# Attention, Fourier mixing and an MLP on one core: q, k and v cast in their transfer by GpSimd's queue, and the second MLP product of all chunks from seven block products

## The chip, the core and the metric

The kernel runs on one core of a Trainium2 chip. The time is the device time of one execution in microseconds (us). A run of the kernel is compared with runs of the kernel before on the same chip.

## The reference, cut to what matters

For 4 batches of 768 positions and 8 heads of 64, a causal attention with a window of 96 and 8 global keys makes x. The real part of a two-dimensional Fourier transform of x is added to it, the rows are normalised, and an MLP of width 2048 is added:

```python
scores = q @ k.T / 8 - slopes[:, None, None] * dist      # dist: |i - j|, 96 for a global key out of the window
a = softmax(where(is_global | is_local, scores, -1e9))
x = (a @ v).transpose(0, 2, 1, 3).reshape(4, 768, 512)
u = x + real(fft(fft(x, axis=1), axis=2))
un = (u - mean(u)) / sqrt(var(u) + 1e-6)
out = u + relu(un @ w_ch1) @ w_ch2                       # w_ch1 [512, 2048], w_ch2 [2048, 512]
```

q, k, v and the two weights are given in fp32; all products are made in fp16 with fp32 sums.

## The kernel before

The order of all work is made at build time by a list scheduler, `Plan` (L23). Work of PE stands in four streams: MIX (the Fourier part), ATT (attention), PH (first MLP product) and PG (second one, taken strictly in order). Work of the other engines and of the DMA queues is handed to `later` with the engines that may do it and an assumed cost for each. `run` (L153) walks through both and always takes what can start first by its own clock, corrected by hand-set offsets (`BIAS`), and by assumed landing times (`LAND`). What comes out is one fixed instruction list for each engine, executed in order, with semaphore waits between engines. DMAs rotate over eight semaphores, so that an issue waits for the eighth one before it.

**Loads.** A head pair's q, k or v is 384 KB in fp32. All 68 such DMAs are issued by the sync engine (SP), in `load` (L362) and `run_dma` (L407). They land as fp32 in buffers that are free for now: those of hT (the hidden activations), u, qs, and for batch 1 those of the weights w1 and w2. An engine then casts each to fp16: q and k in `cast_qk` and `cast_direct` (ACT L411, DVE L413, POOL L415), v of batches 0 and 1 in `cast_v0` (POOL L456), v of batches 2 and 3 in `cast_v` (POOL L501). The weights are loaded by POOL's queue as eight DMAs of 512 KB that cast in the transfer (`wload` L1467, issues L1472 and L1477). A small DMA, `hold` (L1484), stands in SP's queue until the last piece of w2 has landed; the loads of batches 2 and 3 stand behind it.

**Attention.** Keys are kept in an order in which the even positions of a block of 128 come ahead of the odd ones. For batches 0 and 1, `v_place` (L460) brings v into that order by 12 matmuls of 64x128 per head pair (L472), through PSUM, with a copy on DVE (L490) and one on ACT (L491). With two of the units stand 24 matmuls on zeros (L465). q and k are transposed by PE in `trans` (48 transposes of 64x64 per pair, L583; copies DVE L594 or ACT L598) for batches 0 and 1, and by DMA in `trans_dma` (L550; one full and two half transposes per pair, SP) for batches 2 and 3. Scores (`score` L605) of batches 0 and 1 get their distance bias by a matmul (L629) and go through exp (ACT L665). Those of batches 2 and 3 go through exp (L662) and are multiplied by exp of the bias, `mk`, on DVE (L677). `mk` is made by eight exps of a table `dist_k`, which POOL copies (L1431). Products with the global keys (`glob` L711, from `kG`, POOL copies L544) and with v (`av` L750, L765 and L776) follow.

**Fourier part and MLP.** x goes out to DRAM and comes back in another row order (`bounce` L805). The transform is folded and multiplied (`fold_s`, `fold_d`, `y_unit` L987), mirrored by POOL copies (`mirror` L1022 to L1035) and multiplied again (`u_unit` L1067); u is added up by DVE (L1086, L1095), un made by ACT (L1117), 1/std by POOL (L1133, L1134). Per batch there are three chunks of 256 rows, twelve in all. A chunk's first product is `ph_unit` (L1188, 64 matmuls of 256 columns, relu on ACT L1194 or DVE L1195). Its second product is, for the first eight chunks, `pg_unit` (L1212, 32 matmuls of 512 columns; the result is added to u by DVE, L1221). For the last four (`CS = 8`) it is made from seven products of 2x2 blocks instead of eight (`pg_units`, 56 matmuls of 256 columns, L1293; adds L1311). This takes sums of blocks of w2, made once (`w2_sums` L1239), and of hT for each chunk (`s_sums` L1253), all by DVE. The sums stand in space of `mk` and of the exp buffers that batch 3's attention no longer needs.

Of the kernel before, what the change touches and what calls it, by code (L numbers as in the profile page):

```python
# [14 lines left out]
P = 128  # L15
# [7 lines left out]
class Plan:  # L23
# [8 lines left out]
    LAND = {("xw", 0, 0): 34.0, ("xw", 0, 1): 36.0, ("xr", 0): 41.0, ("ld", 4, 2): 47.7, ("ld", 5, 2): 53.4, ("ld", 6, 2): 58.9, ("ld", 7, 2): 64.7, ("w1", 0): 44.6, ("w1", 1): 48.2, ("w1", 2): 52.2, ("w1", 3): 55.8, ("w2", 0): 59.5, ("w2", 1): 63.6, ("w2", 2): 66.6, ("w2", 3): 69.1}  # L32
    LAT = {"ACT": 0.14, "DVE": 0.12, "POOL": 0.08}

    def __init__(self):
        self.t = {"PE": 0.0, "ACT": 0.0, "DVE": 0.0, "POOL": 0.0, "SP": 0.7, "DMA": 1.9, "DMA2": 0.0}
        self.tok = {}
        self.ready = []
        self.pending = []
        self.rings = {}  # L40
        self.left = {}
        self.n = 0
        self.lanes = [0.0] * 8

# [23 lines left out]
    def later(self, ways, needs=(), after=0.0, outs=(), uses=(), ring=None, lat=0.0, dma=0.0, then=None, rank=1, nd=None):  # L68

        self.n += 1  # L70
        if nd is None:
            nd = int(dma > 0 and ways[0][0] in ("SP", "ACT"))
        self.pending.append((self.n, ways, list(needs), after, outs, uses, ring, lat, dma, then, rank, nd))
        self.promote()
# [11 lines left out]
    def first(self):  # L86

        best = None
        for i, (ready, p) in enumerate(self.ready):
            if p[11]:  # L90
                ready = [max(r, self.lanes[p[11] - 1]) for r in ready]
            c = (min(max(self.t[w[0]], r) for w, r in zip(p[1], ready)) - self.AHEAD * (p[10] < 0) + self.BIAS.get(p[4][0] if p[4] else None, 0.0),
# [4 lines left out]

    def emit(self, place):
        ready, (_, ways, needs, after, outs, uses, ring, lat, dma, then, _, nd) = self.ready.pop(place)
        if nd:  # L100
            ready = [max(r, self.lanes[nd - 1]) for r in ready]
# [14 lines left out]
        for _ in range(nd):  # L116
            self.lanes.append(max(end + lat, self.t[eng] + 2.2, *[self.LAND.get(o, 0.0) for o in outs]))
            self.lanes.pop(0)
# [4 lines left out]
        self.promote()  # L123

# [9 lines left out]
    def slot(self, tag):  # L134
# [7 lines left out]
    BIAS = {(1, 5): -0.7, ('ss', 1, 1): -3, (2, 27): -0.7, ('ex', 1, 3, 2): -3, (1, 46): -0.7, ('qk', 10, 1): -1.5, ('c', 't1'): 1.5, ('w1', 2): 3,  # L142
            ('er', 4): -0.7, ('ss', 2, 0): 0.7, ('h', 6, 6): 3, ('qk', 5, 0): 3, ('qkT', 6): -0.7, ('c', 't2'): 0.3, ('ex', 1, 2, 0): -0.7,
            ('xb', 11, 2): -1.5, ('h', 6, 5): 3, ('ss', 2, 1): 0.7, ('qkT', 10): -0.7, ('ex', 0, 2, 1): -1.5, (3, 13): 0.7, (1, 42): 0.7,
            ('un', 7, 0): -0.7, ('s', 11, 3): 0.7, ('x', 0, 3, 2): -1.5, ('qk', 9, 0): 1.5, ('qk', 7, 1): -0.7, ('qk', 0, 0): 1.5,
            ('ld', 15, 1): 1.5, ('h', 5, 1): 0.3, ('h', 5, 4): 0.3, ('qk', 11, 1): 0.7, (3, 73): -1.5, ('un', 0, 1): -1.5, ('y', 1, 2, 0): 3,
            ('er', 2): 0.3, ('qkT', 8): 0.7, ('h', 8, 4): -1.5, ('w1', 0): 3, ('vc', 2): 0.7, (1, 36): 0.3, (3, 47): 0.3, ('ld', 8, 1): -1.5,
            ('ob', 11, 1): -3, ('qkT', 14): 0.7, ('er', 19): -0.3, ('h', 8, 0): -1.5, (1, 92): -0.7, ('kG', 14, 0): 0.3, ('u', 5, 0): 0.3,
            ('w2t', 0): 0.3, ('z', 3, 0): 3, (1, 64): -1.5, ('v', 0, 2, 0): -0.3, ('ss', 6, 1): 3, (2, 21): -1.5, (2, 19): 0.3, ('rd', 10, 0): -0.7,
            ('sid', 2): -0.3, (3, 51): -3, (2, 5): -3}  # L150
    AHEAD = 0.0

    def run(self, streams):  # L153

        left = [[(*u, (i, k)) for k, u in enumerate(s)] for i, (s, _) in enumerate(streams)]
        while True:
            best = None
            for i, s in enumerate(left):
                for k, (needs, ring, _, name) in enumerate(s[:self.LOOK if streams[i][1] else 1]):
# [13 lines left out]
                    c = (max(r, self.t["PE"]) + self.BIAS.get(name, 0.0), i, k, g or "", max(r, self.t["PE"]))  # L173
# [37 lines left out]
def kernel(  # L211
# [63 lines left out]
    sel = np.zeros((P, 128))  # L275
    gpos = np.flatnonzero(tau < NG)
    for h in range(4):
        for g in range(NG):
            sel[gpos[g], h * 32 + h * NG + g] = 1.0
# [37 lines left out]
    NBUF = {"hT": 3, "qk": 2, "qs": 3, "qkT": 4, "er": 2, "v0": 2, "eg": 1, "x": 1, "xr": 1, "zy": 1, "eA": 1,  # L317
# [10 lines left out]
    ident = kon.tile([P, 256], FP16, tag="ident", name="ident")  # L328
    sel_sb = ident[:, 128:256]
    idn = ident[:, 0:128]  # L330
    dist_sb = kon.tile([P, 2, NM], FP16, tag="dist", name="dist")
    dist_k = kon.tile([P, NM], FP16, tag="distk", name="distk")
    sid = kon.tile([P, H, P], FP16, tag="sid", name="sid")
# [3 lines left out]
    mk = kon.tile([P, H, NM], FP16, tag="mk", name="mk")  # L337
    W1 = {}
# [4 lines left out]
    v16 = [kon.tile([P, NS, H, 66], FP16, tag=f"v16{i}", name=f"v16{i}") for i in range(2)]  # L343
# [14 lines left out]
    def vat(n):  # L358

        return ("u", min(n, HP)) if n < HP or n == 2 * HP - 1 else ("qs", 2 + n - HP)  # L360

    def load(b, hp, which):  # L362
        n = HP * b + hp
        h0 = 2 * hp
        gate = [("gate",)] if n == FB * HP else []
        if b >= FB:
            srcs = [(0, q), (1, k)] if which == "qk" else [(2, v)]
            for w, src in srcs:
                i = 1 + HP + 3 * (n - FB * HP) + w

                def run(src=src, i=i, w=w):
                    t = stage[("t", n, w)] = buf("qs", i, [P, 2 * NS, Dh], FP32, 1)
                    if w < 2:
                        run_dma(t.rearrange("p (m t) d -> p m (t d)", t=2), src, b, h0)
                        return
                    x = src[b, h0:h0 + 2].rearrange("h s d -> (h s) d").rearrange("(n m t) d -> t m n d", m=64, t=2)
                    for t2 in range(2):
                        nc.sync.dma_start(t[64 * t2:64 * t2 + 64], x[t2])
                pl.later([("SP", 0.55 if w < 2 else 1.1, run)], free("qs", i) + gate, 0.0, [("ld", n, w)], lat=1.7, dma=1.5 if w < 2 else 2.5, nd=1 + (w > 1))
                if w < 2:  # L380
                    cast_direct(b, hp, w, i)
        elif which == "v":
            def run():
                t = stage[("t", n, 2)] = buf(*vat(n), [P, NS, 2 * Dh], FP32, 1)
                run_dma(t, v, b, h0)
            pl.later([("SP", 0.55, run)], free(*vat(n)) + [("xi",)] * (n >= HP), 0.0, [("ld", n, 2)], lat=1.7, dma=1.45)
        else:
            tag, ti, users, slot = (("hT", hp, 2, 0) if hp < 3 else ("qs", 0, 1, None)) if b == 0 else \
                (("w1", "w2")[hp // 2], 0, 4, 2 * (hp % 2))
            for w, src in enumerate((q, k)):  # L390
                at = (tag, ti) if slot is not None else (tag, w)

                def run(w=w, src=src, at=at):
                    if slot is None:
                        t = buf(at[0], at[1], [P, NS, 2 * Dh], FP32, 1)
                    else:
                        if at not in stage:
                            stage[at] = buf(at[0], at[1], [P, users, NS, 2 * Dh], FP32, users)
                        t = stage[at][:, slot + w]
                    stage[("t", n, w)] = t  # L400
                    run_dma(t, src, b, h0)
                pl.later([("SP", 0.55, run)], free(*at), 0.0, [("ld", n, w)], lat=1.7, dma=1.45)
                cast_qk(b, hp, w, at)

    def run_dma(t, src, b, h0):

        nc.sync.dma_start(t, src[b, h0:h0 + 2].rearrange("h s d -> (h s) d").rearrange("(m p t) d -> p m (t d)", p=P, t=2))  # L407

    def copy_on(on, d, s):
        if on == "ACT":  # L410
            A(d, s, AF.Copy)  # L411
        elif on == "DVE":
            V.tensor_copy(d, s)  # L413
        else:
            nc.gpsimd.tensor_copy(d, s)  # L415

    def cast_qk(b, hp, w, at):
        n = HP * b + hp

        def cast(on):  # L420
            if n not in qk16:
                qk16[n] = buf("qk", n, [P, 2, NP, 2, 2, Dh], FP16, 1)
            d = qk16[n][:, w].rearrange("p n t h d -> p (n t) h d")
            s = stage[("t", n, w)].rearrange("p (h n) (t d) -> p h (n t) d", h=2, t=2).rearrange("p h j d -> p j h d")
            copy_on(on, d, s)
        ways = [("ACT", act(768), lambda: cast("ACT"))]
        if b == 0 and not (w and hp):
            ways.append(("DVE", dve2(768), lambda: cast("DVE")))
        elif b == 0:
            ways = [("POOL", 0.87, lambda: cast("POOL"))]  # L430
        else:
            ways.append(("POOL", 0.87, lambda: cast("POOL")))
        pl.later(ways, [("ld", n, w)] + free("qk", n), 0.0, [("qk", n, w)], [("free",) + at], rank=b)

# [25 lines left out]
    def v_place(b, hp):  # L460
        n = HP * b + hp

        def run(start, ring):
            pv = bank(ring, f"pvp_{n}")
            idle = lambda k: [nc.tensor.matmul(pv[:, 1, 3 * P:4 * P], EG[:, 0:P], EG[:, 0:P], start=True, stop=True) for _ in range(k)]  # L465
            if n == 1:
                idle(10)
# [1134 lines left out]
```

The softmax here doesn't subtract the row's maximum and nothing guards it: scores larger than these inputs give would overflow.

## Time and profile before

| what | value |
|---|---|
| median of 3 runs | 263.72 us (263.44 to 265.83) |
| span of the profiled execution | 263.7 us |
| PE busy | 246.5 us, 93% |
| DVE, ACT, POOL busy | 173.3, 151.4, 67.2 us |
| first MLP product begins (L1188) | 53.1 us |
| last matmul ends | 259.7 us |
| DMA queues of SP and ACT | 57.3% and 6.8% of 16 engines' time |
| DMA queue of POOL (w1, w2) | 9.8% |

A row of a group of instructions reads: line, engine, operation, result<-operands, shape and type, count | busy us, mean ns of one | idle us of the engine just before them, and what ended most of it. PE is the matmul side of TensorE, PEld its weight load, which overlaps. The chain of waits is the work that ended last, followed back from the end; printed in order of time, each piece has its start, its length, its engine and line. A mean of matmuls is longer than their pace, as they overlap; the pace is read from the chain.

### The profile page before, as it was taken

The page shows a single profiled execution, that of the slowest core. Times are in us where ns is not written, and L with a number is a line of the kernel's source. Part 1 is how long each engine was busy: PE and PEld are TensorE (multiplying, and loading weights), DVE is VectorE, ACT ScalarE, POOL GpSimd, SP SyncE. Part 2 cuts the span into 40 slices and gives each one's busy share as a digit, 9 for nine tenths or more (in the row PEclk, how much of TensorE's full clock was granted, in tenths as well). Part 3 has the DMA queues.
Part 4 walks back from the last instruction along what each step waited for, and adds up shares of the span by engine and source line. Part 5 has one row for each costly group of instructions (what it writes and reads, how often), then busy time and mean ns, then how long its engine had stood idle before and what let it go on. Part 6 is the DMA issues. An engine that isn't in the chain of part 4 may idle for free.

```text
span 263.7 us, 7306 instructions
## 1 busy us (share of the span) xinstructions
PE 246.5 (93%) x3080; PEld 180.6 (68%) x3080; DVE 173.3 (66%) x355; ACT 151.4 (57%) x257; POOL 67.2 (25%) x130
## 2 busy tenths in 40 slices
PE   8678778799999999999999999999999999999993
PEld 2556555578765785776685465677678778888883
DVE  3348999853399536782578958578995935644373
ACT  3276999756647655795682364993544265433300
POOL 1334335980041063514101623011221311000000
PEclk9799999979999999999999999999999999999998
DMA  7999959999699998999999897303641440310222
GB/s 211 296 293 272 309 142 289 225 196 201 125 223 172 283 267 106 183 212 157 218 160 207 205 281 116 90 2 82 145 137 40 23 114 25 83 40 2 80 80 82
DMA packets 76386, 42.02 MB, mean 159 GB/s; under 512 B 33474, under 2 KB 72514, under 8 KB 76354
## 3 DMA queue, kind: packets, MB, share of 16 engines
q1 hardware_dynamic: 69298, 32.65, 57.3%
q0 software_dynamic: 4224, 4.19, 9.8%
q10 hardware_dynamic: 2832, 4.72, 6.8%
q8 instruction: 24, 0.39, 0.6%
q14 instruction: 8, 0.07, 0.1%
HBM read 31.59 MB, written 9.44 MB: 156 GB/s over the span
## 4 chain that ended last, share of the span: by engine, by line
PE 77%; ACT 10%; DVE 5%; DMA 2%; issue 1%; POOL 1%; SPq 1%; DVEq 0%
PE ph L1188 30%; PE pg L1212 21%; PE pgD L1293 5%; ACT ex L665 4%; PE pgA L1293 4%; PE pav L776 4%; PE pu L1067 3%; PE py L987 3%; DMA u<-in_v_dram 2%; PE sc L638 2%; DVE qkT L594 2%; ACT er L662 2%; PE pav L765 1%; ACT un L1117 1%; POOL ww L1035 1%
## 5 line engine op out<-in xcount | busy, mean ns | idle before, releaser
L1188 PE MATMUL ph<-unT,w 128*128 128x256 f16 x768 | 94.7, 276 | 0.0
L1188 PEld LDWEIGHTS <-w 128*128 128x128 f16 x768 | 73.9, 99 | 13.9 <-issue 2.2
L1194 ACT ACTIVATE hT<-ph 128x512 f16<-128x512 f32 x81 | 48.1, 599 | 48.4 <-PE ph L1188 48.3
L1212 PE MATMUL pg<-w,hT 128*128 128x512 f16 x256 | 59.9, 379 | 0.0
L1212 PEld LDWEIGHTS <-hT 128*128 128x128 f16 x256 | 24.3, 98 | 24.7 <-issue 0.6
L662 ACT ACTIVATE er<-sc 128x768 f16<-128x768 f32 (+2 forms) x24 | 21.4, 929 | 6.0 <-PE sc L638 5.9
L665 ACT ACTIVATE ex<-sc 128x992 f16<-128x992 f32 (+2 forms) x24 | 20.6, 937 | 2.1 <-PE sc L641 2.1
L677 DVE TENSOR_TENSOR ex<-er,mk 128x768 f16<-128x768 f16 (+2 forms) x24 | 15.6, 661 | 8.1 <-ACT er L662 7.9
L1133 POOL TENSOR_SCALAR sm<-sm 128x2 f32<-128x2 f32 x12 | 4.4, 368 | 62.8 <-ACT un L1126 62.6
L1221 DVE SCALAR_TENSOR_TENSOR u<-pg,sm,u 128x512 f32<-128x512 f32 x16 | 12.0, 748 | 11.8 <-PE pg L1212 11.8
L1086 DVE SCALAR_TENSOR_TENSOR u<-pu,xr 128x512 f32<-128x512 f32 x18 | 11.7, 688 | 9.0 <-PE pu L1067 9.0
L501 POOL CAST v<-qs 128x768 f16<-128x768 f32 x8 | 6.8, 844 | 40.1 <-DMA qs<-in_v_dram 40.1
L1126 ACT ACTIVATE un<-un 128x512 f16<-128x512 f16 x24 | 15.0, 626 | 3.2 <-DMA unT<-un 1.8
L776 PE MATMUL pav<-v,ex 128*128 128x65 f16 x352 | 16.5, 193 | 0.4 <-ACT ex L665 0.3
L776 PEld LDWEIGHTS <-ex 128*128 128x128 f16 x352 | 15.1, 97 | 2.4 <-issue 1.3
L411 ACT ACTIVATE qk<-qs 128x768 f16<-128x768 f32 x11 | 9.2, 844 | 9.6 <-DMA out_dram<-u 7.0
L1035 POOL COPY ww<-zy 128x512 f16<-128x512 f16 x16 | 9.2, 609 | 21.1 <-PE py L987 17.7
L1195 DVE TENSOR_SCALAR hT<-ph 128x512 f16<-128x512 f32 x15 | 10.3, 688 | 6.1 <-PE ph L1188 6.0
L1117 ACT ACTIVATE un<-u,sm 128x512 f16<-128x512 f32 x13 | 9.2, 720 | 8.7 <-DVE sm L1090 8.5
L1293 PEld LDWEIGHTS <-hT 128*128 128x128 f16 x128 | 12.5, 98 | 1.6
L796 DVE TENSOR_TENSOR x<-pav,rc 128x512 f16<-128x512 f32 (+1 forms) x21 | 12.9, 615 | 0.7
L544 POOL COPY kG<-qkT 64x8 f16<-64x8 f16 x32 | 8.1, 256 | 18.9 <-DVE qkT L594 15.0
(124 smaller groups left out, 382.1 us busy)
## 6 DMA issues: line engine op xcount, KB each, us to landing
out_dram<-u SPq DMA_DIRECT2D x23, 256.0 KB, 2.3
w<-in_moe_w_ch_dram POOLq DMA_DIRECT2D x8, 512.0 KB, 11.2
qs<-in_q_dram SPq DMA_DIRECT2D x9, 384.0 KB, 5.2
qs<-in_k_dram SPq DMA_DIRECT2D x9, 384.0 KB, 5.0
qs<-in_v_dram SPq DMA_DIRECT2D x16, 192.0 KB, 5.0
xr<-xd ACTq DMA_DIRECT2D x3, 768.0 KB, 5.3
u<-in_v_dram SPq DMA_DIRECT2D x5, 384.0 KB, 7.1
w<-in_q_dram SPq DMA_DIRECT2D x4, 384.0 KB, 6.7
```

The source lines that it names most:

```text
L662: A(mine(), cut(pa), AF.Exp, 0.0, 0.125)
L665: A(cut(expst[hp][:, :, g * 512:g * 512 + (384 if g == 2 else 512)]), cut(pa), AF.Exp, 0.0, 0.125)
L677: VT(o, mine(), m, op=ALU.mult)
L776: nc.tensor.matmul(po[:, jj, hh * 65:(hh + 1) * 65], lhsT, v16[b % 2][:, i, h, 0:65], start=(jp == 0 and a == 0), stop=(a == len(ops) - 1) ...
L796: VT(X[b][:, 2 * jp:2 * jp + 2, first * Dh:(first + nh) * Dh].rearrange("p j (h d) -> p j h d", d=Dh), pv[:, :, :, 0:Dh], rc.to_broadcast( ...
L1035: nc.gpsimd.tensor_copy(rev[:, n], T[("y", b)][:, n, :, :, ::-1])
L1126: A(x, x, AF.Square, accum_out=MV[c][:, a, 2:3])
L1188: nc.tensor.matmul(ph[:, a * CH:(a + 1) * CH].rearrange("p (x m) -> p x m", x=2), W1[0][:, d, jb * P:(jb + 1) * P], UNT[c][:, :, d, :], st ...
L1194: pl.later([("ACT", act(512), lambda: A(dst, ph, AF.Relu)), ("DVE", dve(512), lambda: V.tensor_scalar_max(dst, ph, 0.0))], [], e, [("h", c ...
L1212: nc.tensor.matmul(pg, HT[c][:, jb, t * P:(t + 1) * P], W2[0][:, jb, :], start=(jb == 0), stop=(jb == NJ - 1))
L1221: V.scalar_tensor_tensor(UT[c][:, t, :], pg, MV[c][:, t, 3:4], UT[c][:, t, :], op0=ALU.mult, op1=ALU.add)
L1293: nc.tensor.matmul(o, lhs(j), rhs(j), start=(first and j == 0), stop=(j == NK - 1), skip_group_check=True)
```

## The change

1. All q, k and v are loaded by DMAs on POOL's queue that cast from fp32 to fp16 and write straight to where the data is used. v comes as two DMAs per head pair, each with every second position into 64 partitions (768 runs of 256 B). q and k of batches 0 and 1 come as one DMA each (768 runs of 512 B, 16 DMAs), those of batches 2 and 3 as four each (384 runs of 256 B, 64 DMAs). With this the staging buffers, all casts, `v_place` with its copies, the 68 loads of SP and `hold` are gone; 24 matmuls on zeros stay (`idle`). A POOL copy of one cell of batch 0's re-read x (`wgate`) stands ahead of batch 1's v and of w2; q, k and v of batches 2 and 3 are issued after w2.
2. A PE transpose takes all 128 partitions (24 instead of 48 per pair); DMA transposes are 16 full ones instead of 8 full and 16 half ones; q and k have three buffers (`NBUF`) and those of hT.
3. `CS = 0`: all twelve chunks use the block products. The two products that take plain blocks come first (p2, p1), then p45, p6, p7, p3. The tables of w2 and two sums of a chunk have space of their own (`wt`, `sx2`) or that of the distance tables (`first`), free after the last `mk` exp; table t1 overwrites a block of w2, sums s3 and s4 overwrite blocks of hT. Each sum may be made by DVE or POOL: of 48 sums of hT 30 stand on DVE and 18 on POOL, of 8 of w2 5 and 3.
4. `LAND` is empty, and `BIAS` has other entries, which also name groups.

```diff
     def load(b, hp, which):
...
-                pl.later([("SP", 0.55 if w < 2 else 1.1, run)], free("qs", i) + gate, 0.0, [("ld", n, w)], lat=1.7, dma=1.5 if w < 2 else 2.5, nd=1 + (w > 1))
...
+        if which == "v":
+            for t in range(2):
+                def run(t=t):
+                    nc.gpsimd.dma_start(v16[b % 2][64 * t:64 * t + 64, h0:h0 + 2, :, 0:Dh].rearrange("m h i d -> m (h i) d"),
+                                        v[b, h0:h0 + 2].rearrange("h (i m t) d -> t m (h i) d", m=64, t=2)[t])
+                pl.later([("POOL", 0.84, run)], ([("avdone", b - 2)] if b > 1 else []) + order_needs(b, "v"), 0.0, [("v", b, hp, t)],
+                         lat=2.2, dma=0.63, rank=order_rank(b, hp, "v"))
+            return
+        tag, ti = ("hT", n // 2) if n < 6 else ("qk", n - 6)
+        for w, src in enumerate((q, k)):
+            if b >= FB:
+                for x in range(4):
+                    def run(w=w, src=src, t=x // 2, h=x % 2):
...
+                        nc.gpsimd.dma_start(qk16[n][64 * t:64 * t + 64, w, :, h], src[b, h0 + h].rearrange("(i m t) d -> t m i d", m=64, t=2)[t])
+                    pl.later([("POOL", 0.5, run)], free(tag, ti) + order_needs(b, "qk"), 0.0, [("qk", n, w, x)], lat=2.2, dma=0.32, rank=order_rank(b, hp, "qk"))
+                continue
...
+                nc.gpsimd.dma_start(qk16[n][:, w].rearrange("p h n t d -> p (h n) (t d)"),
+                                    src[b, h0:h0 + 2].rearrange("h s d -> (h s) d").rearrange("(m p t) d -> p m (t d)", p=P, t=2))
...
     def trans(b, hp):
...
-                        for a in range(2):
-                            for h in range(2):
-                                r = slice(64 * a, 64 * a + 64)
-                                nc.tensor.transpose(o[64 * h:64 * h + 64, a, w, x, t], src[r, w, x, t, h], idn[r, r],
-                                                    tile_position=(64 * a, 64 * h))
+                        for h in range(2):
+                            nc.tensor.transpose(o[64 * h:64 * h + 64, w, x, t], src[:, w, h, x, t], idn,
+                                                tile_position=(0, 64 * h))
...
     def w2_sums(i):
...
+        both([("w2", 2 + i), ("w2", i)], "t3", lambda: WT(1)[:, k0], lambda: b(1, 1), lambda: b(0, 1), ALU.subtract)
+        both([("t3", i)], "t2", lambda: WT(2)[:, k0], lambda: WT(1)[:, k0], lambda: b(0, 0), ALU.add)
+        both([("t2", i)] + [("mk", hp) for hp in range(HP)], "t4", lambda: WT(0)[:, k0], lambda: b(1, 0), lambda: WT(2)[:, k0], ALU.subtract)
+        both([("t3", i)] + [("plain",)] * (pl.CS > 0), "t1", lambda: b(0, 1), lambda: b(0, 1), lambda: b(0, 0), ALU.subtract)
...
     def s_sums(c):
...
+        both(hs + sfree(0), ("s", c, 1), lambda: new(0), lambda: block(1, 0), lambda: block(1, 1), ALU.add)
+        both([("s", c, 1)] + sfree(1), ("s", c, 2), lambda: new(1), lambda: SX[c, 0], lambda: block(0, 0), ALU.subtract, [("free", "sx", 0, i0)])
+        both([("s", c, 1), ("p1", c)], ("s", c, 3), lambda: block(1, 0), lambda: block(0, 0), lambda: block(1, 0), ALU.subtract)
+        both([("s", c, 2), ("p2", c)], ("s", c, 4), lambda: block(0, 1), lambda: block(0, 1), lambda: SX[c, 1], ALU.subtract, [("free", "sx", 1, i0)])
...
+        PG.append((h1 + [("w2", 2), ("w2", 3)], ("pg",), p2))
+        PG.append((h0 + [("w2", 0), ("w2", 1)], None, p1))
+        PG.append(([("s", c, 1)] + tws("t4") + tws("t1"), ("pg",), p45))
+        PG.append(([("s", c, 2), ("lo", c)] + tws("t2"), None, p6))
+        PG.append(([("s", c, 3), ("ra", c, 1)] + tws("t3"), None, p7))
+        PG.append(([("s", c, 4), ("rd", c)], None, p3))
...
         for i in range(8):
-            needs = [("qk", 7, 1), ("free", "w1", 0)] if i == 0 else [("wl", 3), ("free", "w2", 0)] if i == 4 else [("wl", i - 1)]
+            needs = ([("qk", 7, 1, "i")] if i == 0 else [("wl", i - 1)]) + [("wgate",)] * (i == 4)
...
+        pl.later([("POOL", 0.2, lambda: nc.gpsimd.tensor_copy(cell, XR[0][0:1, 0, 0:2]))], [("xr", 0), ("wl", 3)], 0.0, [("wgate",)], rank=pl.ORD["gate"])
```

## The prediction

> **What bounds the kernel now.** I read the page's first two parts, then a table of windows, then the chain of waits in order of time, then the groups.
>
> ```profile
> PE 246.5 (93%) x3080; PEld 180.6 (68%) x3080; DVE 173.3 (66%) x355; ACT 151.4 (57%) x257; POOL 67.2 (25%) x130
> PE   8678778799999999999999999999999999999993
> DMA  7999959999699998999999897303641440310222
> ```
> PE is not full in the first eight slices (to 53 us) and is full after. The transfers fill the same start, and stay high to slice 25.
>
> ```profile
> 0.00:20.00 20.00, 14.49 (x302) 8.58 (x302) 7.85 (x30) 9.25 (x12) 6.09 (x18) 0.91 1.05 267
> 20.00:40.00 20.00, 15.70 (x528) 11.53 (x530) 17.91 (x43) 17.38 (x26) 7.75 (x18) 1.00 0.92 244
> 40.00:60.00 20.00, 17.28 (x287) 12.84 (x285) 15.52 (x32) 15.38 (x34) 15.62 (x25) 0.91 1.16 232
> 60.00:80.00 20.00, 20.00 (x244) 14.92 (x242) 11.17 (x21) 11.87 (x24) 3.50 (x5) 1.00 0.94 185
> ```
> (Window, length, busy PE, weight load, DVE, ACT, POOL, clock, DMA share, GB/s.) From 20 to 40 DVE and ACT are the full engines (17.9 and 17.4 of 20); from 60 PE is.
>
> ```profile
> 2.87 5.53 DMA u<-in_v_dram
> 8.45 0.83 POOL v L456
> 9.32 0.53 PE pvp L472 x12
> 9.86 1.62 PE pvp L465 x14
> 11.50 0.57 DVE v L490
> 12.10 0.49 ACT v L491
> 12.59 1.76 ACT ex L665 x2
> ...
> 52.16 0.62 ACT un L1117
> 53.14 5.26 PE ph L1188 x32
> ...
> 258.81 0.89 PE pgD L1293 x8
> 259.73 0.48 DVE u L1311
> ```
> The start hangs on v's cast and placing, in front of the first exp (12.59); from the first MLP product (53.14) to the last matmul (259.73) the chain is PE almost without a break. So the time is a start S = 53.1, a PE run of 206.6 and a tail of 263.7 − 259.7 = 4.0. The execution's 263.7 is the median's 263.72, so the sum needs no offset.
>
> **What the Trainium skill says.** "DMA: Bandwidth & Descriptors", section "SWDGE vs HWDGE vs iDMA": a cast in the transfer can only be issued by GpSimd, whose cores write every descriptor. The trace agrees that this takes POOL's time: L1472/L1477 issue w in 0.74 to 0.86 us each, for 512 runs.
> "SBUF — State Buffer", "SBUF: two separate sides": while VectorE runs in a two-port mode, GpSimd can't write descriptors, so that such a DMA starves. The trace doesn't show it: four w issues took 2.98 us at 51.6 while DVE had work for 15.5 of 20 us. But those are eight issues; the change has 120.
> "DMA: Bandwidth & Descriptors", "Why small descriptors are slow": 11 cycles for 256 B, 27% of it overhead. The trace has 18.5 ns per 256-B packet per engine (16 engines over 863 packets/us at 112 us) against 27.4 ns for 512 B (5833 packets in 10 to 20), so halved runs cost 1.35 times per byte.
> "GPSIMD Engine Reference", "Elementwise — side-by-side cycle accounting": a two-input add of 2048 fp32 takes 4497 ns on GpSimd, 2293 on VectorE. No such large operation is in the trace.
>
> **The change, part by part.**
> *Second product.* Removed: 256 matmuls of 512 columns (four in 0.86 us on the chain: 215 ns) and 224 of 256 (16 in 1.75: 109 ns) = 55.0 + 24.4 = 79.4. Added: 672 of 256 columns at 109 = 73.2. PE saves 6.2, all after 53 us where PE is the bound.
>
> *v placing.* 96 matmuls and their copies go; 36 of them run after 53 us (three units of some 0.35): 1.0 saved. 24 idle matmuls stay, placed elsewhere. Scores, global rows and transposes move by tenths of a us on PE. So the PE run becomes 206.6 − 7.2 = 199.4.
>
> *Start.* Up to 53 us ACT loses some 7 casts of q/k (L411, 0.84) and 5 copies of v (L491, 0.49) = 8.4; it gains two of the qkT copies (L598, 1.45), so 5.5 net. The first exp no longer waits for the cast, placing and two copies of v: q and k of the first pair landed at 5.5, transposes, copy (0.95) and scores end near 8.5, so 4.1 earlier. What is late next is ACT's own queue: 24 exp (22.5), 3 qkT copies (4.4), the global part (2.4), FFT copies (4.2), un and its transposes (4.7) = 38 from 8.5, thus 46.7 with no idle time. The loads: sixteen 384-KB q/k pieces of 768 packets at 27.4 ns / 16 = 1.3, 21; sixteen halves of v at 0.89, 14 (eight of them behind the w1 loads), each 512-KB piece of w 2.65 (198 GB/s written in the window 58 to 66, where little but w moved), and x out, x back and the FFT tables 768 KB each at the 292 GB/s of 10 to 20: 8.1. Before the first product q/k of two batches, v of batch 0 and half of batch 1, and half of w1 must be in: 21 + 10.7 + 5.3 + 8.1 = 45.1, and some 1.5 to land. So both bounds are 46 to 47; I take S = 48, its ends 44 (some of un after the first product) and 53 (nothing gained).
>
> *DVE.* Loses 3 casts (1.4), 8 copies of v (4.5), some qkT copies; gains 11 sums of 0.69 (30 + 5 against 24) = 7.6, and adds: 48 × 0.46 + 24 × 0.73 = 39.6 against L1221's 12.0 and some 12.6 in L1311, 15. From 53 to 260 it had 135 of 207; some 155 of 200 remain below PE. PE waits for a sum only if it is late: p45 needs s1, t1 and t4, and t4 and chunk 0's s1 need all eight mk exps (0.72 each). I charge 3 us of stalls (ends 0 and 9, the whole saving of the product).
>
> *POOL.* Loses 27 casts of about 0.85 (23); gains 48 issues of 768 runs and 64 of 384, and 21 two-input sums of 128x1024. Issue price from 512 runs in 0.77: if fixed, 0.77 for all; if by run, 1.16 and 0.58. I take 0.85 and 0.6 = 79. A sum: from 1.2 (twice L1035's 0.61 copy of 512) to 2.25 (half the page's figure, an estimate): I take 1.6 = 34. POOL gets 67 − 23 + 79 + 34 = 157, 62%: hidden beside PE, if in time. Its queue is in order: a sum, a mirror (L1022 to L1035) or rstd (L1133) waits behind each issue, and each issue waits for the eighth-last of its kind and, for batches 2 and 3, for a q/k buffer that the transposes of an earlier pair free. Behind a blocked issue stand rstd (adds, then PSUM banks, then PE) and sums (PE itself).
>
> *The gate.* POOL copies a cell of batch 0's re-read x before it issues v of batch 1 and w2; POOL stands until that x has landed (41 us in the trace). Behind it are the distk copies (L1431), which waited for the same x at 41.09, and the first mirrors (46.34): nothing of these gets later. The second half of batch 1's v is issued behind the mirrors, and the last score-value products of batch 1 wait for it: beside MLP products by then, 0 (uncovered, one load, 2 to 3 us).
>
> *SP.* Loses 68 loads, the hold (27 us in which its queue stood) and a third of the transposes' instructions; stores and x move up. It isn't on the chain but for the last store, which stays. Gain 0, and none is needed.
>
> Sum: 48 + 199.4 + 4.0 + 3 = 254.4.
>
> **The rivals.**
> *B, slower: POOL's queue becomes the pace between 50 and 149 us* (batch 3's scores began at 149). In it stand 64 issues of q/k (37 to 51), 24 of v (19 to 28), w2 (3), three mirror sets (10), nine rstd (8), kG copies (4), about nine sums (11 to 20): 92 to 124 us of work for 99 us, before any wait. At the upper end it is 25 late. Half of that can be hidden by MLP work of earlier chunks, the rest stops PE: 254.4 + 12.5 = 267, and with starving as the skill has it more, 272. It decides from an issue of some 0.75 per 384 runs with sums of 2.2. For it: one in-order queue does three kinds of work. Against: w issues didn't stretch beside DVE.
> *C, the start gains nothing*: 256-B runs and one issuing queue make v of batch 1 and w1 late; S = 53: 53 + 199.4 + 4 + 0 to 3 = 256.4 to 259.4. For it: DMA shares of 0.92 to 1.16 up to 60 us. Against: it is faster all the same.
> *D, the block products wait for their sums*: p45, p6, p7, p3 stand in order and the second product is the only filler late on. S = 48 to 50 and stalls of 10: 261.4 to 263.4. For it: t4 and chunk 0's s1 lie where the distance tables were, so no chunk can begin its p45 ahead of batch 1's last attention. Against: DVE at 78% has room, and `ph` products can run ahead by what the hT buffers hold.
>
> **How the numbers follow.** Forecast 0.50 (247 to 258), B 0.27 (267), C 0.11 (258), D 0.12 (262.5). A measurement of this kernel tells about 1% from no change: 261.1 to 266.4. Faster: 0.50 + 0.11 = 0.61; same: D and B's near end, 0.14; slower: 0.25. The range goes from S = 44 without stalls, 44 + 199.4 + 4 = 247, to B's 268, leaving out B's far end (0.13) and 0.05 below. The predicted time is the forecast's.
>
> **What would show it.** First exp near 8.5 us and first ph product at 46 to 50; product groups of 672 matmuls at 109 ns with no idle time before them; PE 97% from then on; POOL near 155 us, an issue of 384 runs at 0.6. Wrong if POOL is busy nine tenths from 50 to 150, or PE idles for a DMA, rstd or a POOL sum: then B. A first ph at 53 is C; idle before the block products released by DVE is D.

## The result and the profile after

The changed kernel takes 301.98 us (298.02 to 303.08, four runs) against 263.85 before: a ratio of 1.138, interval 1.132 to 1.144. The forecast was 254.4. The table of the experiments gives the median and the range of all runs of a kernel, while ratios, and the differences in the text, leave out runs that took over 1.5% longer than the fastest of their kernel (nine of the 21 of g2, for one). The profiled execution has a span of 296.0. Its first part and some slices:

```profile
PE 250.0 (84%) x2976; PEld 202.8 (69%) x2976; DVE 206.3 (70%) x385; ACT 139.7 (47%) x236; POOL 172.6 (58%) x237
PE   8978754899658977799698929999998999999983
POOL 8995307985988599999999970630803441010020
```

ACT's time fell by 12 us. POOL grew from 67 to 173 us, and DVE by 33 us; the terms of the prediction gave it some 15. PE has gaps up to slice 24 where it had been full from slice 9 on. Four windows (columns as in the prediction):

```profile
40.00:60.00 20.00, 12.23 (x176) 9.43 (x174) 7.18 (x19) 9.44 (x23) 12.75 (x21) 0.74 0.95 125
80.00:100.00 20.00, 15.59 (x117) 12.42 (x116) 19.93 (x27) 8.22 (x13) 15.04 (x18) 0.83 0.91 102
120.00:140.00 20.00, 19.86 (x192) 13.56 (x192) 13.79 (x25) 13.13 (x21) 19.36 (x31) 0.85 0.90 93
160.00:180.00 20.00, 12.70 (x98) 10.27 (x97) 18.64 (x24) 5.28 (x8) 15.34 (x12) 0.84 0.78 135
```

From 40 to 60 PE is emptier than before (17.28). From 80 to 100 DVE is without a gap, in only 27 operations. In these four PE's granted clock is low (0.74 to 0.85), in the third with PE busy for 19.86 of 20; what lowers it isn't shown. The chain of waits in order of time:

```profile
29.27 12.73 DMA xd<-x
42.09 4.27 DMA xr<-xd
...
57.50 1.04 PE ph L1083 x8
...
79.11 2.41 DVE ww L741
...
117.95 2.15 POOL sx L1172
120.16 2.63 POOL hT L1172
...
134.40 6.63 POOL qk L398 x10
...
292.44 0.48 DVE u L1207
```

By the prediction's own sum: the start is 57.5 instead of 48, the PE run 292.4 - 57.5 = 234.9 instead of 202.4, the tail 3.6 instead of 4.0. For these 32.5 us, and the 3 of stalls in the forecast, the trace from 60 on shows 27 of idle PE (204.9 busy of 232.4) and, by an estimate from its mean clock of 0.96, 8 of slower work. Three different things stand in the chain: x's write and read-back, VectorE operations of over 2 us, and GpSimd's sums and load issues.

What the VectorE operations are shows in the timeline of DVE and of POOL (start, length, engine, line):

```profile
89.06 3.21 DVE L853 TENSOR_TENSOR ww<-eA 128x256 f16<-128x256 f16 x1
92.19 0.28 DVE L854 TENSOR_TENSOR ww<-eA 128x256 f16<-128x256 f16 x1
92.39 2.21 DVE L855 TENSOR_TENSOR ww<-eA 128x256 f16<-128x256 f16 x1
94.52 0.28 DVE L856 TENSOR_TENSOR ww<-eA 128x256 f16<-128x256 f16 x1
```

```profile
89.96 2.15 POOL L1172 TENSOR_TENSOR first<-hT 128x1024 f16<-128x1024 f16 x1
92.19 2.26 POOL L1172 TENSOR_TENSOR sx<-first,hT 128x1024 f16<-128x1024 f16 x1
```

Four equal additions: two take 0.28, and two last until the end of a sum on GpSimd. (The first had begun 0.9 us before its sum did, beside the issue of a load; why it stood then isn't shown.)

### The profile page after: what moved, and what is told of

Same layout as the page of the kernel before. It is cut to its first block, busy times and chain, and to the rows that moved or that the text cites. A ratio compares the mean times of both kernels' runs of the same rounds, so it can differ in the third digit from the quotient of the medians.

```text
span 296.0 us, 7153 instructions
## 1 busy us (share of the span) xinstructions
PE 250.0 (84%) x2976; PEld 202.8 (69%) x2976; DVE 206.3 (70%) x385; ACT 139.7 (47%) x236; POOL 172.6 (58%) x237
## 3 DMA queue, kind: packets, MB, share of 16 engines
q1 hardware_dynamic: 25136, 13.75, 19.7%
## 4 chain that ended last, share of the span: by engine, by line
PE 36%; DVE 27%; POOL 15%; DMA 6%; issue 5%; ACT 1%; SPq 0%; DVEq 0%; POOLq 0%
PE ph L1083 14%; PE pgA L1188 9%; POOL qk L398 7%; DMA xd<-x 4%; PE pgD L1188 4%; DVE u L1207 4%; PE pu L962 3%; POOL v L386 3%; DVE hT L1170 2%; DVE x L691 2%; PE pav L671 2%; PE py L882 2%; POOL hT L1172 2%; POOL ww L930 1%; DMA xr<-xd 1%
## 5 line engine op out<-in xcount | busy, mean ns | idle before, releaser
L1089 ACT ACTIVATE hT<-ph 128x512 f16<-128x512 f32 x83 | 49.1, 597 | 73.4 <-PE ph L1083 66.5
L1207 DVE SCALAR_TENSOR_TENSOR u<-pgA,sm,u 128x256 f32<-128x256 f32 (+1 forms) x48 | 26.2, 546 | 19.7 <-PE pgA L1188 19.3
L564 ACT ACTIVATE er<-sc 128x992 f16<-128x992 f32 (+2 forms) x24 | 21.7, 924 | 22.0 <-PE sc L539 12.2
L1188 PE MATMUL pgA<-w,hT 128*128 128x256 f16 x192 | 24.7, 279 | 8.2 <-DVE u L1207 8.2
L1172 POOL TENSOR_TENSOR first<-hT 128x1024 f16<-128x1024 f16 x6 | 13.5, 2244 | 23.4 <-PE pgD L1188 14.9
L386 POOL DMA_DIRECT2D v<-in_v_dram x32 | 24.5, 784 | 1.5 <-PE pav L671 1.5
L579 DVE TENSOR_TENSOR ex<-er,mk 128x992 f16<-128x992 f16 (+2 forms) x24 | 19.0, 800 | 5.7 <-ACT er L564 5.7
L398 POOL DMA_DIRECT2D qk<-in_k_dram x32 | 21.1, 676 | 2.7 <-DMA w<-in_moe_w_ch_dram 1.8
L398 POOL DMA_DIRECT2D qk<-in_q_dram x32 | 21.6, 695 | 0.2 <-issue 0.2
L1207 DVE SCALAR_TENSOR_TENSOR u<-pgD,sm,u 128x512 f32<-128x512 f32 (+1 forms) x24 | 14.7, 612 | 7.8 <-PE pgD L1188 7.5
L1021 ACT ACTIVATE un<-un 128x512 f16<-128x512 f16 x24 | 14.9, 623 | 10.1 <-DMA unT<-un 7.2
L1188 PE MATMUL pgA<-wt,sx 128*128 128x256 f16 x96 | 13.3, 284 | 6.6 <-POOL sx L1172 3.3
```

Of the source, the lines that this page charges most:

```text
L386: nc.gpsimd.dma_start(v16[b % 2][64 * t:64 * t + 64, h0:h0 + 2, :, 0:Dh].rearrange("m h i d -> m (h i) d"), v[b, h0:h0 + 2].rearrange("h ( ...
L398: nc.gpsimd.dma_start(qk16[n][64 * t:64 * t + 64, w, :, h], src[b, h0 + h].rearrange("(i m t) d -> t m i d", m=64, t=2)[t])
L564: A(mine(), cut(pa), AF.Exp, 0.0, 0.125)
L579: VT(o, mine(), m, op=ALU.mult)
L1021: A(x, x, AF.Square, accum_out=MV[c][:, a, 2:3])
L1089: pl.later([("ACT", act(512), lambda: A(dst, ph, AF.Relu)), ("DVE", dve(512), lambda: V.tensor_scalar_max(dst, ph, 0.0))], [], e, [("h", c ...
```

## The experiments

Eighteen kernels, each timed beside the kernel before on the same chip (five chips in all, with the kernel before at 263.9 to 264.7). "Same order" means that only the engine of an instruction or its size was changed, not the instruction lists' order; in all others the scheduler laid out the work anew. All but c1 and c2 keep the hand-set offsets (`BIAS`) of the changed kernel, also where other work is laid out. The ratio is to the kernel before, with its 95% interval.

| run | us, median (lowest to highest) | ratio (interval) | first MLP product |
|---|---|---|---|
| changed kernel | 302.0 (298.0 to 303.1) | 1.138 (1.132 to 1.144) | 57.5 |
| e1_sums_dve, same order | 279.8 (277.2 to 281.5) | 1.056 (1.047 to 1.065) | 59.0 |
| i1_no_sums, same order | 275.3 (271.6 to 277.8) | 1.046 (1.042 to 1.051) | 59.3 |
| e2_w1_after_x | 299.3 (295.0 to 299.8) | 1.124 (1.112 to 1.137) | 55.5 |
| e4_two_dmas | 292.2 (291.0 to 292.7) | 1.106 (1.100 to 1.112) | 58.8 |
| c2_after_nobias | 289.8 (289.3 to 296.1) | 1.095 (1.088 to 1.103) | 56.6 |
| f1_dve_32 | 279.1 (278.7 to 279.3) | 1.053 (1.049 to 1.057) | 59.2 |
| f2_dve_16 | 287.9 (285.7 to 291.9) | 1.087 (1.078 to 1.096) | 58.0 |
| f3_dve_w1xr | 279.2 (276.5 to 283.0) | 1.050 (1.043 to 1.057) | 49.1 |
| f4_dve_16_w1xr | 277.3 (276.6 to 278.3) | 1.047 (1.042 to 1.051) | 49.9 |
| g4_cs0_gate3 | 290.4 (289.0 to 293.3) | 1.102 (1.095 to 1.109) | 51.3 |
| e3_loads_only | 285.9 (282.9 to 287.4) | 1.079 (1.070 to 1.087) | 58.5 |
| h2_cs8_w1xr | 278.3 (274.3 to 281.1) | 1.042 (1.033 to 1.050) | 50.4 |
| h1_cs8_16_w1xr | 276.7 (275.9 to 277.8) | 1.047 (1.041 to 1.052) | 49.2 |
| g1_h1_gate3 | 278.7 (276.7 to 279.0) | 1.054 (1.050 to 1.059) | 50.6 |
| g3_h1_nok | 282.3 (275.5 to 283.8) | none | 49.1 |
| g2_h2_gate3 | 264.8 (262.5 to 274.4) | 1.000 (0.997 to 1.003) | 50.2 |
| i2_cs6 | 268.7 (267.2 to 276.8) | 1.016 (1.013 to 1.019) | 49.6 |
| c1_before_nobias | 265.4 (264.7 to 267.3) | 1.004 (1.002 to 1.006) | 54.5 |

### Who makes the sums

The theory: a two-input sum on GpSimd costs its own 2.2 us in an in-order queue, and holds a two-input VectorE operation as long.

```diff
-        G = nc.gpsimd.tensor_tensor
+        G = VT          # in w2_sums and s_sums; the place in the order stays GpSimd's
```

> The changed kernel with its order of work untouched, but the 21 two-input sums that stood on GpSimd are issued on VectorE at the same place. Theory S (each such sum takes 2.2 us of GpSimd's queue and blocks a two-input VectorE operation for as long): 302 falls to 275 to 285; no VectorE product of 128x256 takes over 0.5 us, VectorE busy 206 stays near 200 although it does 21 sums more. Rival Q (the 112 loads issued by GpSimd are the cost): above 292. Rival D (block products wait for their sums, whoever makes them): above 295.

279.8, so some 22 us of the 38 lost are this one choice. The groups of the four additions and of two other lines, in the changed kernel and then in this run:

```profile
L853 DVE TENSOR_TENSOR ww<-eA 128x256 f16<-128x256 f16 x4 | 5.9, 1469 | 0.1
L839 DVE TENSOR_TENSOR eA<-zy 128x1536 f16<-128x1536 f16 x4 | 5.1, 1265 | 0.0
L741 DVE TENSOR_TENSOR ww<-eA 128x1024 f16<-128x1024 f16 (+1 forms) x5 | 4.7, 937 | 0.1
```

```profile
PE 244.1 (87%) x2976; PEld 200.5 (72%) x2976; DVE 191.7 (69%) x406; ACT 139.6 (50%) x236; POOL 123.2 (44%) x216
L853 DVE TENSOR_TENSOR ww<-eA 128x256 f16<-128x256 f16 x4 | 1.2, 292 | 0.1
L839 DVE TENSOR_TENSOR eA<-zy 128x1536 f16<-128x1536 f16 x4 | 3.8, 954 | 0.0
L741 DVE TENSOR_TENSOR ww<-eA 128x1024 f16<-128x1024 f16 (+1 forms) x5 | 2.9, 578 | 0.1
```

VectorE does 21 sums more and is busy for 15 us less. Without those 21 (0.69 each, 14.5) it would have 177.2; in the changed kernel it has 206.3, so 29 us of its busy time there was waiting inside operations. Counted one by one in the trace, 15 two-input operations that met a sum took 26 us more than the shortest of their shape. This is the exclusive lock of the Trainium skill ("SBUF — State Buffer", "SBUF: two separate sides"): of an operation of GpSimd that reads SBUF and one of VectorE with two SBUF inputs, the one that starts first holds the shared ports for its whole length. The trace agrees in its selection too: the adds of L1207, one of whose inputs is in PSUM, take 0.48 for 256 columns in both kernels.

The edit takes away two things at once: 49 us of sums from GpSimd's queue, and the waiting inside VectorE. The waits of PE tell them apart (in all, times, longest), in the changed kernel and then in this run:

```profile
PE pgA L1188 <- DVE u L1207: 12.1, 9, 6.1
PE pgA L1188 <- POOL hT L1172: 3.9, 2, 2.6
PE pgA L1188 <- POOL sx L1172: 3.3, 1, 3.3
```

```profile
PE pgA L1188 <- DVE u L1207: 4.4, 9, 0.9
```

For sums that GpSimd had not finished PE waited 7.2 us. For adds that free its PSUM banks it waited 7.7 more than in this run, and the longest of these waits, 6.1, ends with an add that stands behind held additions:

```profile
171.02 2.09 DVE ww L853
173.10 2.12 DVE ww L854
...
175.63 0.41 DVE u L1207
```

From the first product to the last matmul PE is idle for 27.5 us in the changed kernel (an execution of 298.0) and for 14.3 in this run (one of 281.5): the two waits are about that difference, in equal parts.

Then the sums were taken away as far as a dependence allows, in the same order:

```diff
-            ways = [("DVE", dve2(NK * P), lambda: VT(out(), x(), y(), op=op))]
+            ways = [("DVE", dve2(NK * P), lambda: VT(out()[:, :, 0:2], x()[:, :, 0:2], y()[:, :, 0:2], op=op))]
```

> The changed kernel in its own order, each of the 56 sums cut to two columns of every block on VectorE (the rest of the tables stays as it was, so the block products are of unsummed blocks). Against the run with whole sums on VectorE (279.8, same order) it prices 56 sums of 0.69 = 39 us of VectorE. Theory D (VectorE's sums hold up the products and folds in the middle): 266 to 272. Rival (only the order and the start are left): 276 or more.

275.3: 3 to 5 us less than with whole sums on VectorE, with intervals that overlap, and nearer to the rival than to what was expected. So on VectorE 39 us of sums cost some 5 at most; 21 of them on GpSimd cost 22 more.

### Issuing and short runs

> The changed kernel with q and k of batches 2 and 3 in 32 loads of 768 runs instead of 64 of 384. Heads and positions land in another arrangement, so scores of these two batches are of the wrong pairs; bytes, runs and all later work are the same. GpSimd saves 43 - 24 = 19 us of issuing. Rival Q: 302 falls by 12 or more. Theory S: by 0 to 8, as the sums remain.

```diff
-                for x in range(4):
-                    def run(w=w, src=src, t=x // 2, h=x % 2):
+                for x in range(2):
+                    def run(w=w, src=src, t=x):
...
```

292.2, some 9 less: between the two expectations. The same edit beside sums on VectorE:

> Sums on VectorE (279.8 so measured) and, in addition, q and k of batches 2 and 3 in 32 loads of 768 runs of 256 B, in another arrangement, so that scores of these batches are of the wrong pairs. Theory Q2 (beside the sums, the time in which GpSimd issues loads is the cost from 60 to 160 us): 19 us less issuing give 8 to 12 less, 268 to 272. Rival C (the transfer of 24576 short runs is the cost, however they are issued): within 3 of 280.

279.1 against 279.8: nothing, as rival C said. In these layouts issuing costs only while sums stand in GpSimd's queue too. And fewer, longer runs:

```diff
+                    nc.gpsimd.dma_start(qk16[n][:, w].rearrange("p i h d -> p i (h d)"),
+                                        src[b, h0:h0 + 2].rearrange("h s d -> (h s) d").rearrange("(m p t) d -> p m (t d)", p=P, t=2))
...
```

> As the run before it, but in 16 loads of 768 runs of 512 B: 12288 packets fewer and 30 us of GpSimd's issuing less than with 64 loads; scores of batches 2 and 3 are of wrong pairs. Theory Q2: little more than with 32 loads, 266 to 271. Rival C: 10 or more below the run with 32 loads, under 262.

287.9, slower with 12545 packets fewer than with 32 loads, so rival C falls as well. Neither the number of issues nor that of packets sets the time by itself; the order of work was laid out anew too. Its PE waited 4.7 us for a mirror copy, 3.9 for a fold, and its chain holds two stores of 4.4 and 5.3 us.

### The start

> The changed kernel with the four w1 loads issued only when the last piece of batch 0's x has been normalised (a copy of one cell of it on GpSimd stands ahead of them). Theory W (w1's transfers stand in front of x's write, which took 10 us instead of 4.5, and delay the first MLP product from 48 to 57.5): the write lands in 4 to 5 us, x is back by 41, first product at 49 to 52, time 5 to 8 below the changed kernel, 294 to 297. Rival (the start doesn't count, as GpSimd's queue limits later): within 2 us of 302.

```diff
-            needs = ([("qk", 7, 1, "i")] if i == 0 else [("wl", i - 1)]) + [("wgate",)] * (i == 4)
+            needs = ([("xgate",)] if i == 0 else [("wl", i - 1)]) + [("wgate",)] * (i == 4)
...
+        pl.later([("POOL", 0.2, lambda: nc.gpsimd.tensor_copy(xcell, X[0][0:1, NS - 1, Dm - 2:Dm]))],
+                 [("x", 0, 3, NP - 1), ("qk", 7, 1, "i")], 0.0, [("xgate",)], rank=6)
```

The write took 7.9 and the read-back 7.0, as w1 still ran beside them; first product 55.5, time some 3 less, with intervals that overlap: neither theory is decided. With w1 behind the read-back the write's part is clear:

```diff
-            needs = ([("qk", 7, 1, "i")] if i == 0 else [("wl", i - 1)]) + [("wgate",)] * (i == 4)
+            needs = ([("wgate",)] if i == 0 else [("wl", i - 1)])
...
```

> Sums on VectorE, and w1's four loads and batch 1's v behind the copy of a cell of the re-read x, so that nothing stands with x's write and read-back but batch 1's q and k. Theory W: write 4 to 5 us and read-back 4.5 (12.8 and 5.3 with w1 ahead), x back at 39 instead of 48, first MLP product at 50 to 52 instead of 59, time 272 to 275. Rival (the start is made up later, as other waits pace the middle): 278 or more.

```profile
29.78 4.62 DMA xd<-x
34.48 4.20 DMA xr<-xd
```

x is back at 38.7 and the first product at 49.1, 10 us earlier and 4 earlier than before the change. The time is 279.2, no less, as the rival said: given back in the middle, where PE waits 5.4 us for a fold (L841) and 4.3 for exps. With the loads alone the same edit goes with some 10 us less (ratios of 1.079 and 1.042), in another layout:

> The loads of the changed kernel with the product of the kernel before: block products for the last four chunks only, all sums on VectorE; the scheduler lays out this work anew. Theory S: the loads cost little by themselves, 266 to 274 (57.5 of start, 206 of PE run less 1, 4 of tail). Rival Q: 285 or more, with GpSimd's loads as the wait of PE between 60 and 170.

```diff
-    CS = 0
-    SPOOL = True
+    CS = 8
+    SPOOL = False
...
```

> The loads alone, as the changed kernel has them (64 for q and k of batches 2 and 3), with w1 behind the re-read x: the run of the loads alone (285.9) with its start mended. Theory W: first MLP product at 50 to 52, 276 to 280. Against the run with 16 loads it prices the 48 extra issues and the short runs: Theory Q2 8 to 15 us, its rival 0 to 4.

e3 fell on the rival's side: it is some 21 above the kernel before, with no sum on GpSimd. So the sums are not the only cause. But the rival's mechanism isn't there: from 60 to 160 us PE is idle for 2.3 in all, and for 6.5 from 160 to 180, where POOL is busy for 1.2 of 20. And h2 is no slower than the run with 16 loads (276.7, below): the 48 extra issues cost next to nothing, as Q2's rival said.

### The order

> All three together: sums on VectorE, 16 loads of 512-B runs for q and k of batches 2 and 3 (scores of wrong pairs), w1 behind the re-read x. If sums, issuing and short runs, and the order at the start are the whole of it, the product's saving shows: 254 to 262. If something else in the change costs (the block products' own waits, the order that the scheduler found), 266 or more.

277.3: the three mends together leave 13 us, so something else costs. Two guesses, VectorE and the scheduler's order:

> The run with all three mends (277.3) with block products for the last four chunks only: as in the kernel before, no sum and no extra add stands in the stretch with attention and Fourier folds (scores of batches 2 and 3 are of wrong pairs, from 16 loads). Theory V (VectorE is the bound there once all chunks make their sums on it): 258 to 267. Rival L: 272 or more, as no VectorE work was in the way.

276.7, so taking VectorE's sums out of the middle doesn't help (rival L's side), at least in the order that was found. For the scale, the offsets were taken out of both kernels:

```diff
-    BIAS = {...}
+    BIAS = {}
```

> The kernel before without its hand-set scheduling offsets (BIAS empty), nothing else. It sets the scale for runs whose work the scheduler lays out anew. Theory L (a part of the loss is only an order that doesn't fit): 268 to 276, so that 4 to 12 us of any re-laid run are the order's. Rival: within 2 of 264, and re-laid runs can be read as they are.

> The changed kernel without its hand-set offsets. Theory S: the same causes act, 298 to 312; a time below 295 would say that the offsets themselves are a cost of the change.

265.4 before: 1.004 (1.002 to 1.006), so theory L in this form falls. 289.8 after, with 18 sums on GpSimd: the other outcome that the expectation named, so the changed kernel's offsets, with three sums more on GpSimd, cost it some 11 us. The runs that keep these offsets may carry such a cost too; none of them was made without. Then one place in the order: batch 3's loads behind batch 2's x write.

```diff
-        return [("wl", 7)] if b > 1 else ...
+        return [("wl", 7)] + [("xw", 2, 0)] * (b == 3) if b > 1 else ...
```

> The same order for the loads as the changed kernel has them (64, 256-B runs; 278.3 without it). Theory O: 264 to 272, at most 4 above the run with 16 loads. Rival T: within 3 of 278.3.

264.8, ratio 1.000 (0.997 to 1.003), 11 us below h2: the loads as the change has them, 64 short ones for q and k included, cost nothing on balance once w1 and batch 3 stand elsewhere. The windows in which h2 lost most, in h2 (an execution of 280.1) and then in g2 (one of 269.1), columns as before:

```profile
140.00:160.00 20.00, 16.82 (x133) 9.87 (x132) 15.56 (x33) 7.08 (x8) 5.12 (x12) 0.97 1.10 151
160.00:180.00 20.00, 16.04 (x178) 11.95 (x178) 17.77 (x38) 8.61 (x16) 1.11 (x2) 0.77 0.21 47
```

```profile
140.00:160.00 20.00, 18.96 (x163) 13.51 (x162) 11.80 (x26) 9.92 (x17) 14.81 (x27) 1.00 1.22 129
160.00:180.00 20.00, 19.45 (x165) 12.94 (x164) 9.30 (x18) 11.55 (x19) 13.05 (x25) 1.00 1.38 144
```

The loads gain nothing either, though v's placing, all casts and 3 us of the start are gone. With 16 loads the same edit failed:

> The run with 16 loads, four chunks of block products and w1 behind the re-read x (276.7), with batch 3's loads put behind batch 2's x write in the scheduler's order, so that its attention stands later among the MLP products, about as in the kernel before (first scores of batch 3 after six chunks' first products instead of five). Theory O (the scheduler, free of the hold, pulls batch 3's attention in front and has no MLP work left to hide it: PE idles from 120 to 170): 262 to 270. Rival T (the traffic of the transfers delays reads and stores in the same stretch): within 3 of 276.7.

278.7, where rival T had it. In its chain, and in the waits of PE, stands a load:

```profile
80.12 17.70 DMA v<-in_v_dram
```

```profile
PE pvg L591 <- DMA v<-in_v_dram: 11.8, 5, 4.7
```

A v load of batch 2 took 17.7 us to land, with the DMA share at 1.52 and 1.38 in those windows, and PE stood in its order at the product that needs it. This doesn't decide between order and traffic: the load stood behind others in one queue.

> The run of 276.7 with k of batches 2 and 3 not loaded: its transposes read q instead, so that scores of these two batches are those of q with itself. 3.1 MB and 8 issues fewer in the stretch from 60 to 140; the scheduler may order work around it anew. Theory O: within 4 of 276.7. Rival T: 6 or more less, and reads back of x in 5 us instead of 10.

```diff
-                for x in range(1):
+                for x in range(1 - w):       # k not loaded, its transposes read q
```

282.3 (275.5 to 283.8). Even the fastest run, which is the profiled one, is only 1 us below 276.7, with 3.1 MB fewer, and batch 1's x was read back in 8.6 us (9.4 in h1), not in 5. So rival T's signs are missing. It isn't refuted: from 60 to 80 us the DMA share was 1.57, against 1.52 in h1, so there the edit took no traffic away. A v load took 14.9 us to land in the chain again, and PE waited 3.0 us for v. That the place of a load, and not the traffic, is the limit remains a guess.

### Does the product pay?

> The whole change (64 loads, all twelve chunks by block products) with its sums on VectorE, w1 behind the re-read x and batch 3's loads behind batch 2's x write. Theory O and the product's 6 us together: 262 to 270. If VectorE is the bound once all sums stand on it: 272 or more.

290.4, on the side of the second theory (272 or more). PE's waits:

```profile
PE py L882 <- DVE ww L841: 8.9, 2, 8.2
PE ptu L1053 <- DVE u L981: 3.7, 1, 3.7
```

In this order VectorE's folds of the Fourier part stand behind sums and adds. The milder form, two more chunks at the end of g2:

```diff
-    CS = 8
+    CS = 6
```

> The mended loads (264.8) with six instead of four chunks by block products; the two added ones come at the end, where VectorE has room. Each saves 6.9 - 6.1 = 0.8 us of PE: 263.2 if nothing waits for the eight added sums. Theory D: 266 or more if VectorE is already full there.

268.7, ratio 1.016 (1.013 to 1.019): 3.9 more than g2 instead of 1.6 less. What waits, and the window in which it does:

```profile
PE pgA L1188 <- DVE u L1207: 5.3, 5, 1.6
```

```profile
200.00:220.00 20.00, 17.16 (x178) 15.21 (x177) 18.80 (x41) 3.32 (x4) 3.07 (x7) 1.00 0.33 106
```

VectorE is full there (18.8 of 20), and the next product waits for its add to free the bank. No kernel was found that beats the one before; with all twelve chunks by block products, w1 and batch 3 moved and the offsets taken out, none was run.

## Why the prediction was wrong

**Right.** The block products do take 109 ns per 256 columns (0.87 for eight on the chain). x of batch 0 was ready 4.9 us earlier (its last write was issued by 29.3 instead of 34.2), as the start's "4.1 earlier" said. The first exp began at 9.4, where 8.5 was said. GpSimd's issues cost 0.856, 0.771 and 0.675 by kind, as medians (16 x 0.856 + 32 x 0.771 + 64 x 0.675 = 81.6, against 79), and did not stretch beside a VectorE with 19.9 of 20. v's placing and the casts went as counted. Two counts were off, and nothing hangs on them: SP lost 56 loads, not 68, and one of the eight w issues before took 0.95 instead of 0.74 to 0.86.

**The POOL step failed, and is most of the loss.** "157, 62%: hidden beside PE, if in time" charged nothing of GpSimd's time to others. The size was off too: a sum took 2.1 to 2.86, around the upper bound of 2.25, not 1.6 (POOL 172.6 instead of 157). The step missed that VectorE waits inside its own operations while a sum runs, 29 us of its time, and that PE then waits for adds behind them (7.7 us); and it took sums to be in time for which PE waited 7.2. Shown: 22 us for the choice of the engine, same order; the parts are read from the waits. The prediction named the lock, but applied it only to descriptors, where no effect was seen. The trace before has the other side of it, in small:

```profile
26.20 1.92 POOL L415 CAST qk<-w 128x768 f16<-128x768 f32 x2
27.36 1.17 DVE L841 TENSOR_TENSOR eA<-x 128x768 f16<-128x768 f16 x1
40.87 0.56 DVE L946 TENSOR_TENSOR ww<-eA 128x768 f16<-128x768 f16 x1
```

Beside two casts on GpSimd an addition on VectorE took twice as long as another of its shape.

**Rival B had the place right and the mechanism half.** Its signs came: from 50 to 150 us POOL was busy for 88.8 of 100, and PE idled for POOL's sums. From 100 to 160 the queue was full, with 19.4 to 19.7 of each 20 busy, and stands in the chain. But its price was worked out as queue time alone, to 272 at most, and its point of decision, an issue of 0.75, was not reached (0.675). A full queue by itself isn't the cost: in e1 it has 19.6 and 19.3 of 20 from 100 to 140. It took sums and issues together: less issuing gave some 9 us beside the sums and nothing without them.

**The start step failed.** 45 us of load time were added up as if x's write could take its share at once. Four w1 loads, free to go at 22.9 now that no staging held their buffer, stood in the transfers together with x: the write took 12.7 us (4.6 with w1 behind). So the start was 57.5, 9.5 over. That the gain is real when w1 waits is shown (first product at 49.1 to 51.3 in nine runs); that it shortens the kernel isn't: nothing beside the sums on VectorE (f3), and some 10 us with the loads alone, in a layout that changed with it.

**The stalls of 3 us failed.** "DVE at 78% has room" read a mean over 200 us. In the same order, sums on VectorE cost some 5 us at most; in another order of the whole change (g4) PE waited 8.9 us for folds; and for i2, 5.3 for adds. Rival D's sign is there, block products released by VectorE, but for adds and folds that stand late in its queue, not for VectorE's own late sums (0.9 us in the changed kernel).

**An order was taken for granted.** The sum assumed that the scheduler would keep PE full after the first product. Runs with the same parts lie 11 us apart by one place of loads (h2 and g2), and the changed kernel lost some 11 by its offsets. The terms don't add up to one account: the sums on GpSimd cost 22, those on VectorE 5 at most, and of some 11 left over the kernel before, 6 are the start by the prediction's own sum (59.3 against 53.1), though mending it in f3 gained nothing. The rest, and why some orders stand some 11 us higher than others, were not settled; g1 and g3 point to single late loads, h1 to chains of exps and folds without MLP work beside them.

## What to carry to other kernels

Before moving two-input elementwise work to GpSimd, price it on VectorE's account as well: in the changed kernel every VectorE operation with two SBUF inputs that began while such a sum ran lasted to the sum's end. A load that is made free to go earlier will go earlier: ask which transfer on the critical path it now stands beside, and hold it back with a data dependence. When an in-order program is laid out by a scheduler, compare parts in the same instruction order where that can be had, since a new layout with the same parts moved this kernel by 11 us.

## What the hardware showed that was not expected

A two-input fp16 sum of 128x1024 takes 2.12 us on GpSimd with nothing beside it and up to 2.86 with VectorE at work, against 0.69 on VectorE; a 256-column VectorE addition behind it went from 0.29 to 2.09 and more. Load issues on GpSimd took 0.64 to 0.87 for 384 runs throughout, also from 80 to 100 us where VectorE had no gap. The starving of issues beside VectorE's two-port modes, of which the Trainium skill tells ("SBUF — State Buffer", "SBUF: two separate sides"), wasn't seen; as most of VectorE's work there had two inputs, and no run shows which of it was in such a mode, this is no test of what the page says. Twice the runs cost only 0.10 us more of issuing (0.771 against 0.675).
